# Queue orders, engine sides and bank places of a fused attention and MLP kernel drawn anew

## The chip, the cores and the metric

The kernel runs on one core of one Trainium2 chip. The metric is the device time of one execution in microseconds (us); less is better. The engines are TensorE (PE in the rows, PEld for its weight loads), VectorE (DVE), ScalarE (ACT), GpSimd (POOL) and SyncE (SP). GpSimd and SyncE do no arithmetic here, they issue DMAs: GpSimd those that change f32 into bf16 on the way ("casts"), SyncE the others.

## The reference

Attention with 8 batches, 8 heads, 576 positions, 64 columns a head. Heads 0 to 3 look at a local band, heads 4 to 7 at every 32nd position. Its output, as 4608 tokens by 512, goes through an MLP with a rational function between two products:

```python
mask_local = (rel >= 0) & (rel < 32)
mask_strided = (rel >= 0) & (pos[None, :] % 32 == pos[:, None] % 32)
scores = np.where(masks, q @ k.T / sqrt(64), -1e9)
x = (softmax(scores) @ v).transpose(0, 2, 1, 3).reshape(4608, 512)
h = x @ w_in                                   # 512 x 2048
P = a[0] + a[1] * h + a[2] * h**2 + a[3] * h**3
Q = 1 + abs(b[0]) * abs(h) + abs(b[1]) * h**2
out = (P / (Q + 1e-6)) @ w_out                 # 2048 x 512
```

## The kernel before

`graph` makes a list of 1239 operations in program order; an operation's place in this list is its number ("op 34"). Each names the tiles it reads and writes, from which its waits follow. `place` then takes five written queues, `ORDER`, one for each engine, each a permutation of that engine's op numbers, and `AT`, one digit for each use of PSUM, which gives its bank. `emit` issues every queue in that order with the semaphore waits that the tiles and banks ask for. An engine runs its queue strictly in order: an operation that waits holds up all behind it. `SIDE` is a string of letters, read one by one by `pick`, which say for each eviction, zero fill or `abs` whether ScalarE (a) or VectorE (d) does it. Nothing else decides the order.

**Attention.** Batch 0 is done in two parts, tokens 0 to 255 (part 0) and 256 to 575 (part 1); batches 1 to 7 whole. For batches 0 and 1 GpSimd casts q and k to SBUF, and TensorE turns them ("turn"); later batches are cast to a bf16 copy in DRAM and loaded with transposing DMAs by SyncE. V comes in two forms: vS for the strided heads and vl (tile vL) for the local ones; half of vl is a copy shifted by one block, which for batches from 1 on SyncE makes from the other half ("vsh"). Scores, row maximum, exponential, sum, norm, turn of P, product with V ("sav", "lav"), turn of the local result, and eviction to XT follow.

**MLP.** Ten chunks of tokens: 0 and 1 with 256 tokens each, 2 to 9 with 512 each. A chunk's 2048 middle columns are done in groups, two of 128x4096 elements for most chunks; chunk 0 has two of 128x2048, chunk 1 one of 128x4096, chunk 9 four (4096, 2048, 1024 and 1024 elements wide). "Group 3.0" is the first of chunk 3. For a group TensorE does the W_in steps, ScalarE or VectorE evicts h (L314), then `abs` (ScalarE L1116 or VectorE L1120), u1 and u2 (VectorE, L1123, L1126), ln and exp (ScalarE, L1131, L1136), and p1 to p5 and g (VectorE, L1140 to L1151), so ten long VectorE instructions or nine. W_out steps (L1168), an eviction to `os`, and an output DMA end a chunk.

**Numbers that the text uses.** Casts of GpSimd: 12 to 15 (q, k of part 0), 40 to 43 (q, k of part 1: 40 is q of the local heads), 22 to 25 and 44 to 47 (vS of the parts), 48 to 51 (vl of part 1), 34 and 35 (first and second half of W_in, columns 0 to 1023 and 1024 to 2047), 36 and 37 (halves of W_out), 150 to 153 (q, k of batch 1: 150 is q of the local heads), 210 to 213 (vS of batch 1), 214 to 217 (vl of batch 1). SyncE: 0 to 2 constants, 3 to 5 coefficients a, b and a constant, 218 and 219 vsh of batch 1. VectorE: 6 `babs` (absolute values of b, L308, which every u1 needs), 253 u1 of chunk 1, 1173 the last g. Evictions to XT: 93, 94, 99 (part 0), 320 and 325 (batch 1), 444 and 446 (batch 2), 563 and 565 (batch 3). `abs`: 252 (group 1.0), 363 (2.1), 459 (3.0), 578 (4.0), 939 (7.0), 1111 (9.0). Output evictions: 142 and 148 (chunk 0). TensorE: 144 is the first W_out step of the second 128 tokens of chunk 0; 1184 a pair of W_out matmuls of the last chunk that does not need op 1173 and in the new order stands behind two that do. Fills (L1258) are matmuls of zeros whose result nothing reads.

The casts and the order, in the code:

```python
weights(0, Win[:, :, 0:hw], w_in[:, 0:hw], T_win, "win")              # op 34
weights(1, Win[:, :, hw:2 * hw], w_in[:, hw:2 * hw], T_win, "win")    # op 35
P.op("dve", lambda e: e.scalar_tensor_tensor(coef[:, 6:8], coef[:, 4:6], -1.0, coef[:, 4:6],
     op0=Alu.mult, op1=Alu.max), "tiny", ("babs",), r=[T_co], w=[T_b])   # op 6
for ws, o in queues[e]:           # emit, one engine's queue
    for s, n in ws:
        eng.wait_ge(s, n)
    o.maker(eng).then_inc(o.sem, 16 if o.dma is not None else 1)
```

Of the kernel before, what the change touches and what calls it, by code (L numbers as in the profile page):

```python
# [208 lines left out]
def graph(nc, q, k, v, w_in, w_out, pa, pb, out):  # L209
# [1045 lines left out]
    P.op("dve", lambda e: e.memset(F.bitcast(f32)[:, :], 0.0), "mset64", ("fill", 0), w=[T_f])  # L1255
    for i in range(IDLE):
        BI = Banks(1)
# [5 lines left out]
IDLE = 36  # L1263
# [5 lines left out]
    "daadadadaaaadadaaddddadadaaaaadadaaaaaddaaadadadaaaddddddadaaaaddadaddddaaaadaaadddaaddaaaaaaaaaaaaa"  # L1269
    "aaaadddaaaaaaaaaaaaaaaadddaaaaaaaaaaaaaaaadaaaaaadaaaaaaaaaaaaaaaaaadaaaaaaaaaaadaaaaaadaaaaaaaaaaad"  # L1270
    "aaaaaadaaaaaaaaaaaaaaaaaaaaaaaaaaaadd"
# [24 lines left out]
    ),  # L1296
    "act": (
# [11 lines left out]
    ),  # L1309
    "dve": (  # L1310
# [80 lines left out]
```

## Time and profile before

| | |
|---|---|
| time, median of 3 runs | 353.13 us (352.05 to 354.07) |
| profiled execution, its own time | 349.6 us |
| its span | 347.8 us |
| busy: PE, DVE, ACT, POOL | 324.1, 323.2, 309.3, 74.6 us |
| moved by DMA | 44.68 MB, 128 GB/s |

The profile is one execution, and the span is the time from its first to its last instruction; the profiled execution's own time is a little longer. Busy times are sums over the span and tell nothing of where an engine is idle; the table by stretches does. A row "start us, us, what" gives the start, the length and the work. "Issue" as the cause of a wait means that the profile shows nothing that the engine waited for. "KB each" is what a DMA writes.

### The profile page before, as it was taken

How to read it: one execution, taken by the hardware profiler on the slowest of the kernel's cores; microseconds unless marked ns; L12 is line 12 of the kernel's file. 1: busy time of each engine (PE TensorE's matmuls, PEld its weight loads, DVE VectorE, ACT ScalarE, POOL GpSimd, SP SyncE). 2: the span in 40 equal slices, each digit the busy share in tenths (PEclk: the TensorE clock that was granted, in tenths of full speed). 3: DMA queues.
4: the chain of work that ended last, by engine and by line, in shares of the span. 5: the costliest groups of instructions: out<-in, count | busy, mean ns of one | idle time of the engine just before them, and what ended most of it. 6: DMA issues, size and time to landing. Idle time of an engine off the chain costs nothing.

```text
span 347.8 us, 9956 instructions
## 1 busy us (share of the span) xinstructions
PE 324.1 (93%) x4509; PEld 168.1 (48%) x4552; DVE 323.2 (93%) x291; ACT 309.3 (89%) x273; POOL 74.6 (21%) x112
## 2 busy tenths in 40 slices
PE   5886989999989999999999999999999999999895
PEld 2554667444544454455444454454454444444342
DVE  5783599999999999999999999999999999999994
ACT  8764389699989999899998998999979999999992
POOL 8980052160082062007004170000000000000000
PEclk9997899999999999999999999999999999999999
DMA  9999999995999999699999698701401002001023
GB/s 139 184 178 170 219 142 157 200 172 98 182 204 168 178 208 167 170 176 165 150 235 197 126 134 134 190 30 34 111 2 62 30 2 90 0 30 62 0 90 151
DMA packets 94313, 44.68 MB, mean 128 GB/s; under 512 B 79424, under 2 KB 87360, under 8 KB 93888
## 3 DMA queue, kind: packets, MB, share of 16 engines
q0 software_dynamic: 30528, 18.23, 40.1%
q1 hardware_dynamic: 63200, 25.69, 35.9%
q8 instruction: 35, 0.57, 0.7%
q10 hardware_dynamic: 544, 0.13, 0.2%
q14 instruction: 6, 0.05, 0.1%
HBM read 36.87 MB, written 16.52 MB: 154 GB/s over the span
## 4 chain that ended last, share of the span: by engine, by line
PE 46%; DVE 24%; ACT 15%; DMA 6%; POOL 5%; issue 3%; SPq 1%; DVEq 0%; POOLq 0%
PE ps L1168 19%; PE ps L1098 19%; DMA vL<-in_v_dram 4%; ACT u L1131 4%; ACT h L314 4%; DVE h L1151 4%; DVE u L1126 3%; ACT u L1136 3%; DVE z L1147 3%; DVE u L1123 2%; PE ps L683 2%; DVE z L1143 2%; DVE z L1149 2%; DVE z L1140 2%; DMA consts<-c_cst 2%
## 5 line engine op out<-in xcount | busy, mean ns | idle before, releaser
L1098 PE MATMUL ps<-XT,Win 128*128 128x512 bf16 (+1 forms) x626 | 133.1, 361 | 4.3 <-issue 3.3
L1168 PE MATMUL ps<-Wout,h 128*128 128x512 bf16 x547 | 129.3, 379 | 5.2 <-issue 2.9
L1098 PEld LDWEIGHTS ps<-XT,Win 128*128 128x128 bf16 x640 | 61.1, 99 | 63.7 <-ACT h L314 2.8
L314 ACT ACTIVATE h<-ps 128x1024 bf16<-128x1024 f32 (+1 forms) x78 | 71.2, 956 | 15.5 <-PE ps L1098 15.3
L1168 PEld LDWEIGHTS ps<-Wout,h 128*128 128x128 bf16 x576 | 53.3, 98 | 62.8 <-ACT h L314 1.6
L1131 ACT ACTIVATE u<-u 128x4096 bf16<-128x4096 bf16 (+2 forms) x22 | 66.3, 3012 | 1.1 <-DVE u L1126 1.1
L1136 ACT ACTIVATE u<-u 128x4096 bf16<-128x4096 bf16 (+2 forms) x22 | 66.1, 3010 | 0.1
L1116 ACT ACTIVATE z<-h 128x4096 bf16<-128x4096 bf16 (+2 forms) x16 | 46.0, 2878 | 1.7 <-DVE h L1151 1.3
L1143 DVE TENSOR_TENSOR z<-z,h 128x4096 bf16<-128x4096 bf16 (+2 forms) x21 | 41.5, 1978 | 0.2
L1126 DVE TENSOR_TENSOR u<-u,z 128x4096 bf16<-128x4096 bf16 (+2 forms) x21 | 41.5, 1977 | 0.2
L1147 DVE TENSOR_TENSOR z<-z,h 128x4096 bf16<-128x4096 bf16 (+2 forms) x21 | 41.4, 1979 | 0.2
L1151 DVE TENSOR_TENSOR h<-z,u 128x4096 bf16<-128x4096 bf16 (+2 forms) x21 | 41.4, 1979 | 0.2
L400 POOL DMA_DIRECT2D vL<-in_v_dram x32 | 24.4, 777 | 72.0 <-PE ps L1168 26.1
L391 POOL DMA_DIRECT2D vS<-in_v_dram x36 | 24.9, 708 | 27.0 <-PE ps L1168 18.2
L1123 DVE TENSOR_SCALAR u<-z,coef 128x4096 bf16<-128x4096 bf16 (+2 forms) x21 | 25.0, 1192 | 0.9 <-ACT z L1116 0.7
L1140 DVE TENSOR_SCALAR z<-h,coef 128x4096 bf16<-128x4096 bf16 (+2 forms) x21 | 24.7, 1178 | 0.2
L1145 DVE TENSOR_SCALAR z<-z,coef 128x4096 bf16<-128x4096 bf16 (+2 forms) x21 | 23.4, 1116 | 0.1
L1149 DVE TENSOR_SCALAR z<-z,coef 128x4096 bf16<-128x4096 bf16 (+2 forms) x21 | 23.3, 1117 | 0.1
L314 ACT ACTIVATE os<-ps 128x512 f32<-128x512 f32 x31 | 18.4, 618 | 0.6 <-PE ps L1168 0.6
L683 PEld LDWEIGHTS ps<-ptS,vS 18*64 18x64 bf16 (+1 forms) x1152 | 12.2, 108 | 10.7 <-issue 7.9
L1258 PE MATMUL ps<-F 128*128 128x512 bf16 x36 | 12.1, 426 | 5.1 <-DVE F L1255 4.1
L314 ACT ACTIVATE XT<-ps 128x576 bf16<-128x576 f32 (+7 forms) x30 | 16.1, 572 | 0.3 <-PE ps L1048 0.2
(109 smaller groups left out, 269.7 us busy)
## 6 DMA issues: line engine op xcount, KB each, us to landing
out_dram<-os SPq DMA_DIRECT2D x32, 256.0 KB, 2.5
qk<-in_k_dram POOLq DMA_DIRECT2D x12, 288.0 KB, 7.1
qk<-in_q_dram POOLq DMA_DIRECT2D x12, 288.0 KB, 6.6
Win<-in_moe_w_in_dram POOLq DMA_DIRECT2D x2, 1024.0 KB, 15.8
Wout<-in_moe_w_out_dram POOLq DMA_DIRECT2D x2, 1024.0 KB, 24.3
vS<-in_v_dram POOLq DMA_DIRECT2D x28, 72.0 KB, 5.7
vL<-in_v_dram POOLq DMA_DIRECT2D x28, 72.0 KB, 5.7
vL<-vL SPq DMA_DIRECT2D x14, 138.1 KB, 3.9
```

What stands on the lines that cost most here:

```text
L314: return lambda e: e.tensor_copy(o_(), i_()) if e_ == "dve" else e.activation(o_(), i_(), AF.Copy)
L1098: r = e.matmul(bank(ph, 512 * (s - s0) + n * i, n), Win[:, kk, f * 128:(f + 1) * 128], XT[:, kk, x0:x0 + n], start=(kk == 0), stop=(kk == ...
L1116: P.op(e_, lambda e, z=z, h=h, i=i, hp=hp: e.activation(z.t[:, hp * i:hp * i + hp, :], h.t[:, hp * i:hp * i + hp, :], AF.Abs), f"act_{hp * ...
L1123: dv(lambda e, z=z, u=u, G_=G_: e.tensor_scalar(u.t[:, 0:G_, :], z.t[:, 0:G_, :], b1_ap, b0_ap, op0=Alu.mult, op1=Alu.add), "ts2", "u1", r ...
L1126: dv(lambda e, z=z, u=u, G_=G_: e.tensor_tensor(u.t[:, 0:G_, :], u.t[:, 0:G_, :], z.t[:, 0:G_, :], op=Alu.mult), "tt", "u2", r=[z], m=[u])
L1131: lns.append(P.op("act", lambda e, u=u, i=i, hp=hp: e.activation(u.t[:, hp * i:hp * i + hp, :], u.t[:, hp * i:hp * i + hp, :], AF.Ln, bias ...
L1136: exs.append(P.op("act", lambda e, u=u, i=i, hp=hp: e.activation(u.t[:, hp * i:hp * i + hp, :], u.t[:, hp * i:hp * i + hp, :], AF.Exp, sca ...
L1140: dv(lambda e, z=z, h=h, G_=G_: e.tensor_scalar(z.t[:, 0:G_, :], h.t[:, 0:G_, :], a_ap[3], a_ap[2], op0=Alu.mult, op1=Alu.add), "ts2", "p1 ...
L1143: dv(lambda e, z=z, h=h, G_=G_: e.tensor_tensor(z.t[:, 0:G_, :], z.t[:, 0:G_, :], h.t[:, 0:G_, :], op=Alu.mult), "tt", "p2", r=[h], m=[z])
L1147: dv(lambda e, z=z, h=h, G_=G_: e.tensor_tensor(z.t[:, 0:G_, :], z.t[:, 0:G_, :], h.t[:, 0:G_, :], op=Alu.mult), "tt", "p4", r=[h], m=[z])
L1151: dv(lambda e, z=z, h=h, u=u, G_=G_: e.tensor_tensor(h.t[:, 0:G_, :], z.t[:, 0:G_, :], u.t[:, 0:G_, :], op=Alu.mult), "tt", "g", r=[z, u], ...
L1168: r = e.matmul(bank(po, 0, Fout), hf[:, j, m * 128:(m + 1) * 128], Wout[:, kk, :], start=(kk == 0), stop=(kk == NF - 1))
```

## The change

All five queues, the letters of `SIDE` and the digits of `AT` are replaced; four fills are added (`IDLE`). The operations, their tiles and their sizes are those of before. In GpSimd's queue op 34 moves from the 25th place to the 19th: what stood ahead of it and now stands behind are 152 and 150 (q of batch 1), 40, 48, 49, 51, 217, 211 and 212; what now stands ahead are 44, 45 and 47. Op 35 moves from the 32nd place to the 25th, op 36, the first half of W_out, from the 35th to the 36th, behind op 37 and all V of batch 1. In SyncE's queue 5, 4 and 3 move ahead of 218. 44 of the 237 letters differ; among them `abs` 363, 459, 578 and 1111 go from ScalarE to VectorE, 252 and 939 from VectorE to ScalarE, and nine evictions of 576 columns to ScalarE. The diff, cut to the heads of the queues:

```diff
-IDLE = 36
+IDLE = 40
...
     "pe": (
-        "1225 1208 1234 1226 1231 1216 1232 1218 1215 1219-1220 63 61 1233 1236 1224 66-68 56 58 70 1206 1222 "
-        "1238 1211 159 79 161 80-81 232 164-165 230 1204 83 166 1213 156 85 87 168 1235 77 95 154 227 224 "
-        "1207 1230 1212 75 177 1210 1221 175 89 178-179 222 91 237 181 98 173 1237 185 183 1205 90 220 92 193 "
-        "234 106 292 104 198 293-294 102 296 188 100 1203 187 190 189 121 119 249-250 123 305-307 301 125 303 "
-        "246 309 247 316 311 318 1228 313 243-244 321 240-241 324 326 315 317 138 354 334-335 355 331-332 337 "
...
+        "1224 1208 1238 1222 1242 1216 1226 1239 1205 1213 1212 1236 1228 1232 1241 1209 1221 56 58 1206 1217 "
+        "1214 1231 1220 79 1211 1234 1237 63 80 1207 81 61 234 1229 66-67 83 68 156 85 70 237 161 159 87 1210 "
+        "77 1227 1225 75 164 95 165 1203 166 98 224 168 89-92 1230 1223 102 104 100 154 106 177 175 178 173 "
+        "179 227 230 188 232 125 181 190 119 185 183 220 193 222 121 123 198 305 187 189 306 249-250 307 240 "
+        "292 309 241 293-294 243 246 296 244 247 144 313 311 138 321 145-146 301 303 147 315 139 317 324 316 "
...
     "act": (
-        "31 27 10 207 16 203 9 55 28 65 33 32 39 57 38 71 160 163 233 84 157 88 169 78 155 225 53 223 176 93 "
...
+        "31 27 19 33 57 59 38 9 39 235-236 84 71 158 86 200 160 238 88 225 169 94 103 53 101 155 108 231 126 "
...
     "dve": (
-        "18 17 7 21 20 11 201 19 1202 209 202 208 204-205 64 62 54 29 206 69 200 59-60 8 72-73 162 82 231 167 "
-        "74 86 158 96 170-171 226 97 172 76 228 180 239 52 238 174 194 196 195 197 236 235 107 199 295 103 "
-        "298 6 299-300 192 191 109-110 113-116 308 117 304 127-129 312 132 314 133 322-323 118 325 252-254 "
...
+        "21 209 18 7 1202 203 206 205 54 10 17 16 204 11 202 20 28 32 29 60 8 207 65 64 82 62 69 72-73 163 74 "
+        "55 157 239 78 162 76 96 208 97 167 226 99 170 93 52 6 105 171-172 107 176 174 201 180 109 228 110 "
+        "113 186 114 194 196 115 195 197 116 199 117 127-129 132 308 133-135 295 136 118 137 298 312 299-300 "
+        "322-323 302 253-254 320 257 142 148 258 418 259-261 421-422 262 429 423 341-342 345-347 363-364 "
...
     "pool": (
-        "15 14 12-13 42-43 25 211 152 41 40 212 46 151 150 50 23-24 51 49 48 22 153 217 34 216 47 214-215 45 "
-        "44 35 213 210 36-37 284 286 285 276 275 283 282 278-279 277 400 407 409 406 281 280 399 398 408 401 "
...
+        "12-13 44 15 14 153 41-43 46-47 24-25 151 50 45 23 22 34 48 152 51 49 40 35 216-217 150 212 37 213 "
+        "215 211 210 214 36 278 286 284 275 283 276 279-280 285 277 398 407 400 409 281 406 408 399 282 401 "
...
     "sp": (
-        "30 26 0 2 1 218 5 219 4 3 288-289 291 287 290 424 412 433 410 414 411 413 143 149 268 543 529 552 "
...
+        "30 26 5 0-1 4 2-3 218-219 289 291 288 287 290 143 424 412 433 411 410 414 413 149 531 552 274 533 "
```

## Rows read from the trace of the kernel before

**Rows 1.** The page, busy time (share of the span) x instructions of each engine.

```profile
PE 324.1 (93%) x4509; PEld 168.1 (48%) x4552; DVE 323.2 (93%) x291; ACT 309.3 (89%) x273; POOL 74.6 (21%) x112
```

**Rows 2.** The table by stretches: stretch, its length, busy time of each engine in it, granted TensorE clock, DMA share, GB/s.

```profile
30.70:37.50 6.80, 6.80 (x127) 5.01 (x128) 2.75 (x7) 1.61 (x4) 0.00 (x0) 0.50 1.18 197
37.50:44.60 7.10, 6.32 (x229) 4.78 (x228) 4.57 (x9) 4.33 (x5) 0.00 (x0) 1.00 1.28 221
44.60:62.80 18.20, 16.73 (x325) 12.81 (x323) 17.82 (x22) 16.18 (x17) 7.19 (x10) 1.00 1.07 148
62.80:342.00 279.20, 270.66 (x3343) 132.01 (x3384) 276.38 (x206) 264.12 (x214) 43.97 (x62) 1.00 0.67 118
```

**Rows 3.** The chain that ended last, up to 64 us: start, length, what. L473 is op 218, L308 op 6, the L1123 at 62.83 op 253.

```profile
18.87 14.54 DMA vL<-in_v_dram
33.42 0.76 SPq L473
...
36.10 6.57 DMA consts<-c_cst
...
42.69 0.16 DVE coef L308
...
62.83 1.36 DVE u L1123
```

**Rows 4.** Four casts of GpSimd, asked one by one: the issue (its length in ns, its start in us) and the time from its start to the landing, in us. The first cast of all; the first half of W_in; the second; the last half of W_out.

```profile
L383 POOL DMA_DIRECT2D XT<-in_k_dram x1: 758/758/758, 1.2 to 1.2; - x1
...
DMA to landing us min/median/max: 4.4/4.4/4.4
...
L478 POOL DMA_DIRECT2D Win<-in_moe_w_in_dram x1: 919/919/919, 16.2 to 16.2; - x1
...
DMA to landing us min/median/max: 13.7/13.7/13.7
...
L478 POOL DMA_DIRECT2D Win<-in_moe_w_in_dram x1: 948/948/948, 20.6 to 20.6; - x1
...
DMA to landing us min/median/max: 17.8/17.8/17.8
...
L478 POOL DMA_DIRECT2D Wout<-in_moe_w_out_dram x1: 1084/1084/1084, 23.4 to 23.4; - x1
...
DMA to landing us min/median/max: 26.5/26.5/26.5
```

**Rows 5.** The DMA issues: out<-in, engine, operation, count, KB each, median us to landing. XT is the staging place of q and k of batch 0 (128 KB part 0, 160 KB part 1; k has rows of the same size), h that of batch 1; vS of 32 and vL of 40 KB are those of the parts (vS of part 1 has 40 KB too), those of 72 KB belong to whole batches (vL has rows of the same size).

```profile
Win<-in_moe_w_in_dram POOLq DMA_DIRECT2D x2, 1024.0 KB, 15.8
...
vS<-in_v_dram POOLq DMA_DIRECT2D x28, 72.0 KB, 5.7
...
h<-in_q_dram POOLq DMA_DIRECT2D x2, 288.0 KB, 8.1
...
XT<-in_q_dram POOLq DMA_DIRECT2D x2, 160.0 KB, 6.5
...
XT<-in_q_dram POOLq DMA_DIRECT2D x2, 128.0 KB, 5.0
...
vL<-in_v_dram POOLq DMA_DIRECT2D x4, 40.0 KB, 7.2
...
vS<-in_v_dram POOLq DMA_DIRECT2D x4, 32.0 KB, 7.3
```

**Rows 6.** The timeline of TensorE: start, length, the W_in steps of 256 columns, x matmuls.

```profile
33.48 1.90 PE L1098 MATMUL ps<-XT,Win 128*128 128x256 bf16 x8
...
44.37 3.01 PE L1098 MATMUL ps<-XT,Win 128*128 128x256 bf16 x26 [0.38 <-DVE XT L314]
```

**Rows 7.** The waits of TensorE from 24 to 62.8 us: who, for what, us in total, times, longest.

```profile
PE ps L604 <- issue: 2.4, 1, 2.4
PE ps L1098 <- issue: 0.8, 1, 0.8
```

**Rows 8.** The groups of instructions by line and form, of VectorE and ScalarE: xcount | busy us, mean ns of one | idle before. L1120 and L1116 are `abs` on either engine, L314 an eviction of a bf16 and one of an f32 bank, L1147 p4 and L1145 p3 of a group of 2048.

```profile
L1120 DVE TENSOR_SCALAR z<-h 128x4096 uint16<-128x4096 uint16 x5 | 6.1, 1227 | 1.0 <-ACT h L314 0.9
...
L1147 DVE TENSOR_TENSOR z<-z,h 128x2048 bf16<-128x2048 bf16 x3 | 3.7, 1223 | 0.1
...
L1145 DVE TENSOR_SCALAR z<-z,coef 128x2048 bf16<-128x2048 bf16 x3 | 2.2, 749 | 0.0
...
L314 DVE COPY XT<-ps 128x576 bf16<-128x576 bf16 x5 | 2.2, 449 | 0.0
...
L314 DVE COPY os<-ps 128x512 f32<-128x512 f32 x1 | 0.7, 679 | 0.0
...
L1116 ACT ACTIVATE z<-h 128x4096 bf16<-128x4096 bf16 x11 | 39.9, 3629 | 1.1 <-DVE h L1151 0.9
```

**Rows 9.** The timeline of VectorE in the steady part: p1 of one group, p2 that reads it, u1 of another group, and p3 that does not read that u1.

```profile
287.36 1.34 DVE L1140 TENSOR_SCALAR z<-h,coef 128x4096 bf16<-128x4096 bf16 x1
288.74 2.29 DVE L1143 TENSOR_TENSOR z<-z,h 128x4096 bf16<-128x4096 bf16 x1
290.94 1.34 DVE L1123 TENSOR_SCALAR u<-z,coef 128x4096 bf16<-128x4096 bf16 x1
292.20 1.28 DVE L1145 TENSOR_SCALAR z<-z,coef 128x4096 bf16<-128x4096 bf16 x1
```

**Rows 10.** The timeline of TensorE after the last g: the last W_out matmuls, x matmuls.

```profile
342.06 2.12 PE L1168 MATMUL ps<-Wout,h 128*128 128x512 bf16 x9 [0.21 <-DVE h L1151]
```

More of the change, by code (lines that the diff above doesn't have):

```diff
@@ L1268 @@
 SIDE = (
-    "daadadadaaaadadaaddddadadaaaaadadaaaaaddaaadadadaaaddddddadaaaaddadaddddaaaadaaadddaaddaaaaaaaaaaaaa"
-    "aaaadddaaaaaaaaaaaaaaaadddaaaaaaaaaaaaaaaadaaaaaadaaaaaaaaaaaaaaaaaadaaaaaaaaaaadaaaaaadaaaaaaaaaaad"
-    "aaaaaadaaaaaaaaaaaaaaaaaaaaaaaaaaaadd"
+    "dadddadddaaadaddaaddddddaadadaaddaaaaadddadaaddddadaadadddddaaaddaaaaaadaaaaaaadadaaddaaaaaaaaaaadaa"
+    "aaaadaaaaaadaaaaaaaaaaadaaaaaadaaaaaaaaaaadaaaaaadaaaaaaaaaaaaaaaaaadaaaaaaaaaaadaaaaaaaaaaaaaaaaaad"
+    "aaaaaadaaaaaaaaaaaaadaaaaaaaaaaaaaadd"
 )
@@ L1338 @@
 AT = (
-    "1754500741153050067233777212510325060775164037066465145010432260530510532723203027602304664423306046"
-    "5666620440510030557522020246701205242466616201674016325234320461601427451533354626421465155003570730"
-    "76037016406252502274546211130324755113260"
+    "6340664177065467200320603321217474210056536755046234227524311752240014337006500025300234600763652540"
+    "4001664244102111413664426022273020405340356006452102512465325530611047046322644626246371032504532624"
+    "536527212421637352413274147246235576066337402"
 )
```

81 rows, old and new, of the table ORDER are left out of this document.

## Prediction

> **What bounds the kernel now.** I read the page first, then a table by stretches, then the chain that ended last, then the landings of GpSimd's casts. The page gives VectorE 323.2 us, 93% of the span [rows 1], an average over unlike stretches. The table [rows 2] splits it. From 62.8 to 342 VectorE works 276.38 of 279.20 us and TensorE 270.66: VectorE is the bound, TensorE close behind, and VectorE idles 2.8 us in all. From 44.6 to 62.8 it works 17.82 of 18.20. So the end is settled by two things: when VectorE's unbroken run starts, and how much work it then has. Before 44.6 it idles for long (in the 13.9 us from 30.7 on it works 7.3).
>
> Why so late? The chain [rows 3] answers: a cast of the second batch's V issued at 18.87 lands at 33.4; SyncE, waiting for it with op 218, only then gets to the coefficient loads 5, 4 and 3 behind it, whose last lands at 42.67; `babs` (op 6) follows on VectorE at 42.69, and from there the chain stays on VectorE and ScalarE up to 62.83, where u1 of chunk 1 (op 253) starts. I use op 253 as the milestone: all that varies much in this change lies ahead of it.
>
> **GpSimd's queue.** The casts land nearly in the order of issue, so a landing is the KB ahead of it over a pace. In the kernel before, the first cast lands at 1.2 + 4.4 = 5.6 and the first half of W_in at 16.2 + 13.7 = 29.9 [rows 4]. Between them lie 3 x 128 + 4 x 160 + 4 x 288 KB of q and k, 4 x 32 + 40 + 2 x 72 of the strided V, 4 x 40 + 72 of the local V, and the half itself, 1024: 3744 KB in 24.3 us, 154 KB/us [rows 4, 5]. From there to the last half of W_out (23.4 + 26.5 = 49.9) it is 3552 KB in 20.0 us, 177 KB/us. In the new order 17 casts with 1768 KB lie between the first cast and W_in's first half, then 568 KB (40, 152, 48, 51, 49) up to the second half:
>
> - first half: 5.6 + 2792/154 = 23.7 (was 29.9); second half: 23.7 + 1592/177 = 32.7 (was 20.6 + 17.8 = 38.4);
> - later than before: q of part 1 (op 40) at 27, q of the second batch (op 150, behind both halves) at 32.7 + 432/177 = 35.1, the last of the second batch's local V at 35.1 + 1456/177 = 43.3 (was 33.4), and W_out's first half, now last of all, at 43.3 + 1024/177 = 49.1, near the old end of 49.9, since the sum of the KB is the same.
>
> **The way to op 253 in the new order.** The coefficient loads now stand third, sixth and eighth on SyncE, ahead of 218, and wait for nothing: that wait goes. W_in's first half is there at 23.7, which is about when attention part 0 can deliver the 256 tokens (evictions 93, 94, 99; I walk its queues to 24 or 26). The first three W_in steps follow; the fourth stands behind the turn of op 40, so u1 of chunk 0 starts near 32 instead of 44.6. It does not run on unbroken: the other half of chunk 0 waits for W_in's second half. From 32.7 TensorE is the limit. To the last W_in step of chunk 1 its queue holds 12 steps of eight matmuls, 0.93 each (26 in 3.01 us [rows 6]), 11.1 us; some 18 short steps (masks, scores, turns, V products), which I put at 5 us; and waits of about 4 us (the turn of op 150 at 35.1, exponentials and evictions on ScalarE between the two turns of part 1). That gives 52.8. Then two evictions and one of P on ScalarE, 2.1 us, and `abs` of chunk 1 (op 252), which moves from VectorE to ScalarE, 3.63 instead of 1.23 [rows 8]: 58.5.
>
> What this walk lacks is TensorE waiting for nothing that the profile shows: 2.4 and 0.8 us between 24 and 62.8 [rows 7]. At zero, op 253 starts at 58.5; with all 3.2 us on the path, 61.7. As part falls in stretches that wait for data anyway, I take 2 us: 60.5, which is 2.3 us ahead of 62.83. VectorE has the room: ahead of op 253 the new order gives it some 4.5 us more (zero fills and casts taken from ScalarE), in time that it idles now. If that cover went, they would cost those 4.5 us.
>
> **What VectorE has left from op 253 on.** Added: `abs` of groups 2.1, 3.0, 4.0 and 9.0 at 1.23 each, +4.9 [rows 8]; an eviction of an f32 bank moved behind (op 148, 0.68 [rows 8]) and one moved from ScalarE (op 320; no row of that form; between 0.45 for bf16 and 0.68, I take 0.65). Removed: `abs` of 7.0, -1.23; five evictions of 576 columns (325, 444, 446, 563, 565) to ScalarE, -2.25 at 0.45; and the second half of chunk 0 (p3, p4, p5, g), now done ahead of op 253, -3.9 (p3 and p5 0.75 each, p4 and g 1.22 each [rows 8]). Sum -1.1. Against that, 34 instructions instead of 27 now read what the instruction right ahead wrote. Such a pair costs 0.12 more from start to start (287.36 to 288.74 against 290.94 to 292.20, 1.38 and 1.26 [rows 9]): +0.8. The remainder is the same to 0.3 us, -0.3. ScalarE gets some 8 us less in all; as it idles in this stretch already, that counts for nothing.
>
> **Tail.** After the last g (op 1173) one more pair of W_out matmuls is left in the new order (op 1184), 2 x 0.24 [rows 10]: +0.4. The four added fills stand in TensorE's queue where it waits for casts or evictions, and I take nothing for them; without that cover they cost at most 4 x 0.24 = 1 us.
>
> **Sum.** -2.3 - 0.3 + 0.4 = -2.2 us. The profiled execution took 349.6 us (span 347.8), 1% under the median of 353.13; 349.6 becomes 347.4, and 353.13 becomes 350.9.
>
> **The rivals.** One can't tell less than 0.5%, 1.8 us, from no change.
>
> *The start is repaid (no change).* The KB are the same, so what comes sooner at W_in comes later at q, k and V of the second batch, whose turns stand in TensorE's queue between the W_in steps. With the full 3.2 us of stalls on the path op 253 starts at 61.7, the sum is -1.1 - 0.3 + 0.4 = -1.0 us, and the time 352.1. For it: the last landing stays near 50, and VectorE is 98% busy from 44.6 on already. Against it: VectorE's long idling before 44.6. The Trainium skill ("DMA: Bandwidth & Descriptors", section "Issuing engines are not separate DMA queues") says that DMAs of all issuing engines run on the same 16 DMA engines and interleave; read strictly, an order buys no transfer time, and the gain would be nothing, 353.1. The trace agrees as to the sum of the landings, but its chain shows VectorE held up by a coefficient load of 1 KB behind a wait, which an order can mend.
>
> *W_out comes too late (slower).* In the new order the first W_out step, op 144, stands in TensorE's queue ahead of the turns and the V product of the second batch, and needs the half of W_out that is now last. I have TensorE there at 53 and the landing at 49.1. At the slower pace of 154 KB/us from 23.7 on, the 4504 KB behind W_in's first half land at 52.9; a tenth slower still, at 56.1. Each us past 53 holds `abs` of chunk 1 and op 253 by one. From 53 + 2.2 + 1.8 = 57 on the change is slower by over 0.5%: at 58, 353.13 - 2.2 + 5 = 355.9.
>
> *The clock falls at the wrong time (between).* Before, the granted clock was 0.50 from 30.7 to 37.5 [rows 2], after TensorE had stood still for 2.4 us [rows 7]; eight matmuls took 1.90 us in it [rows 6]. If such a stretch of 6.8 us falls after 32.7, where TensorE is now the limit, it costs up to 3.4 us: 350.9 + 3.4 = 354.3, no change.
>
> *More than expected (faster).* With no stall on the path op 253 starts at 58.5, -4.2; with a lighter ScalarE VectorE may also lose half of its 2.8 us of idle time: 347.6.
>
> **How the numbers follow.** Forecast and its faster neighbour, a gain of over 1.8 us: 0.51 (of that 0.13 for over 4). No change, by repayment, by the clock or by a different loss of the same size: 0.30, of which 0.04 for the strict rule. Slower: 0.19 (late W_out 0.09; the rest a new wait between the second batch's later V and TensorE, or banks redrawn badly, which the trace before cannot show; TensorE's 8.5 us of idle time after 62.8 [rows 2] bounds what banks can give back). The time is that of the likeliest, 350.9. The range runs from 347, the gain without stalls, to 355.5, W_out landing near 57.5.
>
> **What would show it.** W_in's halves landing near 24 and 33, the last of W_out near 50; no wait of VectorE for a coefficient load; u1 of chunk 0 near 32; op 253 (the first 4096-wide u1) at 58.5 to 62; from there to the last g 277 to 279 us, with VectorE idle under 4 us; the clock at 0.50 before 33 or not at all. Wrong it is if TensorE waits for W_out at op 144, if the clock is at 0.50 between 33 and 53, or if VectorE idles over 5 us after op 253.

## The result and the profile after

The changed kernel takes 354.12 us in the median of 20 runs, the kernel before 353.16 in as many of its own: 1.0 us more. The ratio is 1.0056 with a 95% interval of [1.0032, 1.0081], by which it is 2.0 us slower, a little over the 1.8 that the prediction could tell from no change. The ratio, here and below, leaves out executions more than 1.5% above the fastest of the same kernel, while the medians take all, and the execution profiled after is one of those left out. The forecast was 2.2 us faster.

The profiled executions lie further apart than the medians: 349.6 us before (3.5 under its median) and 356.47 after (2.3 over). The span grew by 354.0 - 347.8 = 6.2 us, more than the kernels differ. What is said of the size of the loss goes by the ratio and the medians, 1 to 2 us; the profiles say where time went in these two executions.

From the page after, the busy times and the queue that carries the engines' instructions (packets, MB, share):

```profile
PE 331.8 (94%) x4556; PEld 168.2 (48%) x4556; DVE 327.5 (92%) x293; ACT 302.6 (85%) x271; POOL 74.8 (21%) x112
...
q8 instruction: 35, 0.57, 0.7%
```

VectorE has 4.3 us more of work than in [rows 1]. The table by stretches answers [rows 2]. It is cut where TensorE stops and starts again (24.63, 26.41, 31.30, 35.31), at u1 of chunk 0 (42.03), at op 253 (67.16) and at the end of the last g (347.95). Columns as in [rows 2]: length, busy time and instructions of PE, PEld, DVE, ACT, POOL, granted clock, DMA share, GB/s.

```profile
0.00:24.63 24.63, 18.78 (x349) 9.94 (x349) 17.85 (x42) 12.83 (x20) 18.25 (x33) 1.00 1.18 161
24.63:26.41 1.78, 0.17 (x22) 0.07 (x10) 1.32 (x3) 0.57 (x1) 1.78 (x3) 1.00 1.75 138
26.41:31.30 4.89, 4.83 (x127) 3.47 (x127) 1.33 (x4) 2.26 (x3) 3.83 (x6) 0.74 1.37 195
31.30:35.31 4.01, 0.34 (x2) 0.00 (x0) 1.45 (x3) 0.00 (x0) 0.00 (x0) 0.89 1.90 103
35.31:42.03 6.72, 6.72 (x127) 4.80 (x128) 2.80 (x6) 3.75 (x4) 0.00 (x0) 0.75 1.35 192
42.03:67.16 25.13, 23.29 (x437) 16.51 (x435) 24.29 (x34) 22.95 (x25) 6.23 (x10) 1.00 1.09 133
67.16:347.95 280.79, 274.86 (x3509) 132.33 (x3507) 277.05 (x204) 259.02 (x218) 44.70 (x62) 1.00 0.65 119
```

The kernel before, cut at the same events (u1 of chunk 0 at 44.61, op 253, the last g):

```profile
0.00:21.30 21.30, 15.97 (x348) 9.42 (x348) 15.26 (x37) 17.28 (x25) 20.25 (x36) 1.00 1.22 161
21.30:27.70 6.40, 4.60 (x130) 2.77 (x128) 5.05 (x10) 4.05 (x6) 3.23 (x5) 1.00 1.43 189
27.70:44.61 16.91, 13.80 (x360) 10.19 (x361) 7.32 (x16) 6.52 (x10) 0.00 (x0) 0.80 1.40 197
44.61:62.82 18.21, 16.74 (x325) 12.81 (x324) 17.81 (x22) 16.17 (x17) 7.19 (x10) 1.00 1.07 149
62.82:342.01 279.19, 270.64 (x3343) 132.00 (x3384) 276.38 (x206) 264.12 (x214) 43.97 (x62) 1.00 0.67 118
```

Three readings. First, op 253 starts 67.16 - 62.82 = 4.3 us later, the rest to the last g takes 280.79 - 279.19 = 1.6 more, the tail 0.3 more: 6.2. Second, VectorE's work ahead of op 253 grew from 15.26 + 5.05 + 7.32 + 17.81 = 45.4 us to 49.0, and its idle time there did not shrink: 62.82 - 45.4 = 17.4 before, 67.16 - 49.0 = 18.1 after. Third, TensorE all but stops after 349 + 349 = 698 matmuls and weight loads for 1.8 us, and 254 later, after 952, for 4.0 us. Behind each stop the clock is at 0.50:

```profile
28.80:32.20 3.40, 2.84 (x14) 1.70 (x12) 1.13 (x3) 1.88 (x2) 1.44 (x2) 0.50 1.75 171
35.60:39.00 3.40, 3.40 (x29) 2.11 (x28) 0.15 (x1) 1.30 (x2) 0.00 (x0) 0.50 1.31 201
```

The chain, which answers [rows 3], shows the second stop as "issue", a wait for nothing that the profile shows:

```profile
24.80 1.62 issue
...
28.07 3.57 PE ps L1098 x19
31.64 3.67 issue
35.31 1.00 PE ps L1098 x5
```

The rows x19 and x5 are the first three W_in steps, eight matmuls each. The stop cuts through the middle of the third; no operation of the program begins there. [Rows 7] has the like of it, 2.4 and 0.8 us; here it is 3.7 and 1.6. The kernel before, too, stops after 475 + 476 = 951 instructions:

```profile
0.00:27.66 27.66, 20.57 (x475) 12.14 (x476) 20.31 (x46) 21.33 (x31) 23.49 (x40) 1.00 1.27 167
27.66:29.77 2.11, 0.00 (x1) 0.09 (x1) 0.00 (x0) 0.00 (x0) 0.00 (x0) 1.00 2.34 125
```

### The profile page after: what moved, and what is told of

Read it like the earlier page. It is cut to its first block, busy times and chain, and to the rows that moved or that the text cites. A ratio compares the mean times of both kernels' runs of the same rounds, so it can differ in the third digit from the quotient of the medians.

```text
span 354.0 us, 10000 instructions
## 1 busy us (share of the span) xinstructions
PE 331.8 (94%) x4556; PEld 168.2 (48%) x4556; DVE 327.5 (92%) x293; ACT 302.6 (85%) x271; POOL 74.8 (21%) x112
## 4 chain that ended last, share of the span: by engine, by line
PE 56%; DVE 26%; ACT 12%; issue 3%; DMA 2%; DVEq 0%; SPq 0%
PE ps L1098 23%; PE ps L1168 21%; ACT u L1136 3%; DVE h L1151 3%; ACT u L1131 3%; DVE z L1143 3%; PE ps L683 3%; DVE z L1147 3%; ACT h L314 2%; DVE z L1140 2%; DVE u L1126 2%; DMA qkT<-qk 2%; DVE u L1123 2%; DVE qkT L314 1%; DVE z L1149 1%
## 5 line engine op out<-in xcount | busy, mean ns | idle before, releaser
L1098 PE MATMUL ps<-XT,Win 128*128 128x512 bf16 (+1 forms) x640 | 136.1, 363 | 5.0 <-issue 3.7
L1168 PE MATMUL ps<-Wout,h 128*128 128x512 bf16 x576 | 135.3, 379 | 3.4 <-ACT os L314 1.3
L314 ACT ACTIVATE h<-ps 128x1024 bf16<-128x1024 f32 (+1 forms) x78 | 71.8, 973 | 16.7 <-PE ps L1098 16.5
L1116 ACT ACTIVATE z<-h 128x4096 bf16<-128x4096 bf16 (+2 forms) x14 | 38.6, 2762 | 3.9 <-DVE h L314 1.8
L1147 DVE TENSOR_TENSOR z<-z,h 128x4096 bf16<-128x4096 bf16 (+2 forms) x21 | 41.5, 1981 | 0.2
L400 POOL DMA_DIRECT2D vL<-in_v_dram x32 | 22.2, 697 | 49.7 <-PE ps L1168 44.3
L314 ACT ACTIVATE XT<-ps 128x576 bf16<-128x576 bf16 (+7 forms) x34 | 19.2, 589 | 8.8 <-PE ps L683 7.3
L1123 DVE TENSOR_SCALAR u<-z,coef 128x4096 bf16<-128x4096 bf16 (+2 forms) x21 | 24.9, 1187 | 0.4 <-ACT z L1116 0.2
L1145 DVE TENSOR_SCALAR z<-z,coef 128x4096 bf16<-128x4096 bf16 (+2 forms) x21 | 23.6, 1126 | 0.1
L314 ACT ACTIVATE os<-ps 128x512 f32<-128x512 f32 x30 | 18.5, 638 | 1.7 <-PE ps L1168 1.6
L450 POOL DMA_DIRECT2D qk<-in_k_dram x12 | 8.9, 743 | 43.3 <-PE ps L1098 23.8
L314 ACT ACTIVATE qkT<-ps 64x576 bf16<-64x576 bf16 (+6 forms) x16 | 10.0, 640 | 8.3 <-PE ps L563 4.4
```

The lines of the kernel that those rows point to most:

```text
L314: return lambda e: e.tensor_copy(o_(), i_()) if e_ == "dve" else e.activation(o_(), i_(), AF.Copy)
L1098: r = e.matmul(bank(ph, 512 * (s - s0) + n * i, n), Win[:, kk, f * 128:(f + 1) * 128], XT[:, kk, x0:x0 + n], start=(kk == 0), stop=(kk == ...
L1116: P.op(e_, lambda e, z=z, h=h, i=i, hp=hp: e.activation(z.t[:, hp * i:hp * i + hp, :], h.t[:, hp * i:hp * i + hp, :], AF.Abs), f"act_{hp * ...
L1123: dv(lambda e, z=z, u=u, G_=G_: e.tensor_scalar(u.t[:, 0:G_, :], z.t[:, 0:G_, :], b1_ap, b0_ap, op0=Alu.mult, op1=Alu.add), "ts2", "u1", r ...
L1147: dv(lambda e, z=z, h=h, G_=G_: e.tensor_tensor(z.t[:, 0:G_, :], z.t[:, 0:G_, :], h.t[:, 0:G_, :], op=Alu.mult), "tt", "p4", r=[h], m=[z])
L1168: r = e.matmul(bank(po, 0, Fout), hf[:, j, m * 128:(m + 1) * 128], Wout[:, kk, :], start=(kk == 0), stop=(kk == NF - 1))
```

## The experiments

Two theories at the start. **Supply**: TensorE stops because its instructions have not come; they come in blocks of 256 by DMA, among the casts. **Work**: VectorE has more to do, and when it starts matters little. A third question is what the coefficients were worth.

**The changed kernel, profiled again.** No edit.

> The changed kernel once more, for a second look at the same program: if the standstills are a property of the order, TensorE again stands still after its 698th and 952nd instruction, for 1.5 to 2.5 and 3 to 5 us, op 253 starts at 66 to 68, and from it to the last g it takes 279 to 281 us.

One row of its table by stretches, from 31.90 on:

```profile
31.90:35.02 3.12, 0.27 (x3) 0.00 (x0) 1.69 (x3) 0.80 (x1) 0.00 (x0) 0.91 1.66 105
```

It stops at the same places for 2.3 and 3.1 us, op 253 starts at 68.04, and the rest takes 280.0. Two kernels further down have the same start, since their edits come behind op 253: the one with small matmuls at its end and the one with four `abs` moved back. There u1 of chunk 0 starts at 37.3 and 40.1, op 253 at 65.7 and 66.2. So four profiles of this start have op 253 at 65.7 to 68.0, where the kernel before has 62.8 and, with its coefficient loads moved, 64.3. The late start belongs to this order. The standstills belong to the places in the count, their lengths vary. From op 253 to the last g the changed program took 280.8, 280.0 and, with the small matmuls behind it, 278.9 us: the 1.6 us more than before are not shown to belong to it.

The earliest of the four, from u1 of chunk 0 to op 253:

```profile
37.33:65.66 28.33, 25.74 (x437) 18.16 (x435) 24.56 (x34) 23.25 (x26) 6.23 (x10) 0.88 1.14 147
```

Its stops are shorter (1.1 and 1.0 us, and 1.7 at the next border, right behind u1), but the clock is at 0.50 from 38.6 to 45.4: with u1 4.7 us earlier, op 253 is only 1.5 us earlier.

**GpSimd held back.**

```diff
+    P.ops[35].deps[P.ops[92]] = 1
     P.place({e: list(_expand(t)) for e, t in ORDER.items()}, [int(x) for x in AT])
```

> The changed kernel, with one added wait: GpSimd issues the second half of W_in (op 35), and so all casts behind it, only when TensorE is through op 92 (the last V product of part 0, at 27.4). The casts ahead of it have landed by 28.3, so the DMA engines then have little to do until op 35's data move. Theory of supply: the block of instructions that came at 33.5 now comes before 30.5, TensorE stands still after its 952nd instruction for under 1.5 us instead of 4.1, and u1 of chunk 0 starts at 35 to 38 instead of 42.0; the second half of W_in lands some 5 us later (39), so the end can go either way. Rival: the standstill has another cause (a bank, a weight load, the cast of op 40): then it stays at 3.5 us or more at the same place.

Its table by stretches, cut at its own 698th instruction (24.64), 951st (28.37), u1 of chunk 0, op 253 and the last g, and then a stretch of low clock (the row from 24.64 to 28.37 is left out):

```profile
0.00:24.64 24.64, 19.57 (x347) 10.17 (x351) 17.82 (x42) 12.83 (x20) 15.30 (x28) 1.00 1.16 160
...
28.37:33.89 5.52, 5.23 (x126) 3.77 (x123) 4.53 (x9) 4.66 (x5) 5.52 (x9) 1.00 1.13 191
33.89:64.46 30.57, 26.49 (x438) 18.44 (x439) 24.74 (x34) 23.11 (x25) 6.80 (x11) 0.89 1.32 166
64.46:344.12 279.66, 274.50 (x3509) 132.26 (x3507) 277.02 (x204) 259.03 (x218) 45.60 (x62) 1.00 0.65 119
37.20:40.60 3.40, 3.40 (x49) 2.32 (x47) 0.41 (x1) 2.35 (x5) 0.00 (x0) 0.50 1.27 205
```

Both standstills are gone, and u1 of chunk 0 starts at 33.9, earlier than expected. The rows by DMA queue show what changed (packets, MB, time of the packets as a share of 16 engines, over 100% where packets overlap). First the changed kernel in the 5.5 us after its 698th instruction, then in the 1.65 after those (where the packet that ends the second stop runs), then the held kernel in the 2 us after its 698th:

```profile
q0 software_dynamic: 1446, 1.03, 146.2%
q14 instruction: 1, 0.01, 0.4%
```

```profile
q8 instruction: 1, 0.02, 5.7%
```

```profile
q0 software_dynamic: 377, 0.11, 53.4%
q8 instruction: 1, 0.02, 3.1%
```

In the changed kernel no packet of TensorE's queue (q8) runs from 26.41 to 31.95, while the casts (q0) keep the DMA engines at 146%; it runs after 31.95, and TensorE goes on at 35.31. With the casts held it runs within 2 us, before TensorE needs it. The page gives 35 such packets in 0.57 MB, 16 KB each, for 9112 matmuls and weight loads, 260 to a packet, and the stops lie 254 of those apart (a few instructions of the sequencer are not counted in them): blocks of about 256 instructions. The Trainium skill ("Runtime: NRT & Kernel Launch", section "Instruction fetch mechanics") has those sizes, 16 KiB blocks of 256 instructions fetched by a DMA queue of the sequencer's own, and calls the cost mostly hidden. The trace agrees as to the size; hidden it is not, with 4.0 us at one border.

The hold has its price. TensorE now waits 2.7 us for W_in's second half (landed 36.3, was 34.1), its clock falls to 0.50 in the stretch shown and again from 47.5 to 50.9, and op 253 starts at 64.5. Median 353.44 against 354.37 of the kernel before, ratio 1.0042 [1.0004, 1.008]: the earlier u1 bought little.

**The same, but sooner.** The wait is on op 89 instead of 92.

> As the kernel that held GpSimd at op 35 until TensorE was through op 92, but only until it is through op 89, two to three us earlier (24.8). Theory of supply: the block of instructions asked for at 24.6 is still ahead of the half of W_in and comes at 26.5 to 28; no standstill over 1 us at the 952nd instruction; u1 of chunk 0 at 33.5 to 36; the second half of W_in lands at 33.5 to 35 instead of 36.3, and op 253 starts at 61 to 63.5 instead of 64.5 (67.2 in the changed kernel). Time 2 to 4 us below the changed kernel. Rival: the later steps are held by something else (ScalarE, the half clock): op 253 stays at 64 to 66 and the time within 1 us of the other gate.

Its table by stretches, cut as above, and one stretch of low clock:

```profile
24.63:31.14 6.51, 5.39 (x148) 3.74 (x137) 2.50 (x7) 2.74 (x5) 4.72 (x7) 0.74 0.72 100
...
36.47:61.72 25.25, 23.48 (x438) 16.62 (x436) 24.34 (x34) 23.04 (x26) 6.24 (x10) 1.00 1.39 186
61.72:344.45 282.73, 276.28 (x3509) 133.09 (x3507) 277.32 (x204) 258.94 (x218) 44.94 (x62) 0.99 0.65 118
92.50:95.90 3.40, 3.40 (x43) 1.66 (x43) 2.50 (x4) 1.59 (x1) 0.00 (x0) 0.50 1.27 161
```

U1 of chunk 0 starts at 36.5, op 253 at 61.7, 5.4 us ahead of the changed kernel, as supply has it. The place of the 952nd instruction has no stop; one of 1.1 us is left at the 698th. In this execution the hold was not the sooner one: behind that stop the second half of W_in went out at 26.4 (26.1 with the wait on op 92) and landed at 36.1. What differs is that TensorE came to it later, had no wait for it, and kept its clock at 1.00 from 31.1 to 61.7.

But the span is 352.0, only 2.0 less. From op 253 to the last g it takes 282.7, 1.9 more, and the tail is 1.5 longer. The place of the first, in its chain:

```profile
...
84.32 6.34 DMA qkT<-qk
...
90.70 0.42 PE ps L620 x2
```

TensorE, now earlier, waits 1.8 us for the third batch's q and k, whose load (op 412) stands on SyncE behind the transposing of P (op 424); then its clock is at 0.50 from 92.5 to 95.9. Median 353.11 against 354.04, ratio 1.0014 [0.9975, 1.0054].

**That load moved forward**, with the same hold:

```diff
-        "30 26 5 0-1 4 2-3 218-219 289 291 288 287 290 143 424 412 433 ...
+        "30 26 5 0-1 4 2-3 218-219 289 291 288 287 290 143 412 424 433 ...
```

> The kernel with the gate at op 89, and on SyncE the load of the third batch's strided q and k (op 412) ahead of the transposing of the second batch's P (op 424) instead of behind it. In the trace of the gated kernel TensorE waits for op 412's load from 88.9 to 90.7, the granted clock then falls to 0.50 from 92.5 to 95.9, and VectorE is idle 5.4 us from op 253 to the last g, where the first gated kernel had 2.6. Theory: op 412 is issued at 80 to 82 instead of 84.3, the wait and the half clock go, and the time falls by 1.5 to 3 us below the kernel with the gate alone, under the kernel before. Rival: op 424's transposing, now later, holds TensorE's product of P and V instead, and the time is the same or up to 2 us longer.

From its chain:

```profile
87.49 2.24 issue
89.73 0.46 PE ps L683 x32
```

The rival came: op 412 goes out at 83.3 (80 to 82 were expected), and op 424, now behind it, lands at 89.6; TensorE, which has come to the product of P and V (L683), stands still up to 89.73, and the clock is at 0.50 from 90.0 to 93.4. Of 283.3 us from op 253 on VectorE idles 6.2. The median is 352.42 against 354.01, ratio 0.9968 [0.9923, 1.0014]: the lowest of the study, not told apart from the kernel before. SyncE needs 2.7 to 2.9 us to issue the one load and 1.3 to 2.3 for the other, and at this point both are wanted at once.

**Supply without casts.** In the changed kernel, 640 small matmuls of zeros behind everything else:

```diff
+    for i in range(16):
+        BI = Banks(1)
+        def tiny(e, BI=BI):
+            for _ in range(40):
+                o = e.matmul(bank(BI, 0, 8), F[:, :], F[:, 0:8], start=True, stop=True)
+            return o
+        P.op("pe", tiny, "idle", ("tiny", i), r=[T_f], w=[BI])
```

> The changed kernel with 640 more matmuls of zeros (8 columns each, nothing reads them) behind the last W_out matmul, 1280 more instructions of TensorE, five blocks of 256, at a time when no cast moves. It measures the supply by itself; its own time is of no interest. Theory of supply: in the cast phase a block started no sooner than 5.2 to 8.9 us after the one before. If the casts are what makes the blocks late, TensorE gets through 256 of these in 3.5 to 5.5 us here, with standstills under 2 us. If blocks are always this slow, it stands still at each of the borders and 256 of them take 7 us or more.

Two blocks of them in its table by stretches (a few instructions that straddle a cut are counted twice):

```profile
350.34:353.60 3.26, 3.26 (x134) 3.26 (x132) 0.00 (x0) 0.00 (x0) 0.00 (x0) 0.85 0.03 5
353.60:357.02 3.42, 3.42 (x134) 3.42 (x132) 0.00 (x0) 0.00 (x0) 0.00 (x0) 0.50 0.02 5
...
```

256 instructions pass in 3.4 us, block after block, with TensorE busy throughout. In the cast phase the changed kernel needed 1.78 + 4.89 = 6.7 and 4.01 + 6.72 = 10.7 us for as many, larger ones, and stood still for 1.8 and 4.0 of them. Without casts no block was late.

**Fewer fills.** 30 of the 33 fills ahead of op 106 left out (they compute nothing):

```diff
-IDLE = 40
+IDLE = 10
-        "1224 1208 1238 1222 1242 1216 1226 1239 1205 1213 1212 1236 1228 1232 1241 1209 1221 56 58 1206 1217 "
+        "56 58 79 63 80 81 61 234 66-67 83 68 156 85 70 237 161 159 87 77 75 164 95 165 1203 166 98 ... "
```

> The changed kernel, with 30 of the 33 fills that TensorE's queue has ahead of op 106 (the fourth W_in step of chunk 0) left out. In the trace of the changed kernel TensorE stands still for 1.8 us after 698 and for 4.1 us after 952 of its matmuls and weight loads, with nothing that it waits for; in the kernel before it stands still after 951 too. Theory of supply: its instructions come in blocks of 256 by a DMA that queues among the casts (16 KB packets of the queue called instruction, one at 32.01, just ahead of the restart), so the place of the standstill is a place in the count. With 60 instructions fewer all four W_in steps of chunk 0 come ahead of it: u1 of chunk 0 starts at 33 to 37 instead of 42.0, the standstill comes right behind op 106, op 253 starts 2 to 6 us earlier, and the time falls by 1 to 4 us. Rival, the clock: without fills TensorE is idle for longer, the granted clock is at 0.50 ahead of 28 us, and the time rises. Rival, VectorE's work alone: the start matters little, the time stays within 0.7 us.

Its table by stretches, from the start to each of two stops:

```profile
0.00:26.02 26.02, 14.77 (x346) 10.10 (x349) 17.91 (x42) 12.82 (x20) 18.72 (x34) 1.00 1.18 165
0.00:41.18 41.18, 27.43 (x603) 19.16 (x603) 25.80 (x57) 19.61 (x28) 23.64 (x40) 0.92 1.32 167
```

The two long stops (2.7 and 3.9 us) come after 695 and 1206 instructions, 511 apart: places in the count, 60 instructions further on in the work. At the border between there is no stop; TensorE came to it late enough, it seems, for the block to be there. For the time I was wrong. u1 of chunk 0 starts at 40.1 instead of 33 to 37, op 253 at 69.5, and the median is 359.05 against 354.37, ratio 1.0225 [1.0149, 1.0301]. The rival of the clock came. These are the same masking matmul of 512 columns (op 83) at 14.3 us in the changed kernel, and at 14.4 without fills; the third row is one of the same form in the changed kernel's stretch at 0.50:

```profile
14.32 0.39 PE L782 MATMUL ps<-ng,IDN 128*128 128x512 bf16 x1
```

```profile
14.41 0.61 PE L782 MATMUL ps<-ng,IDN 128*128 128x512 bf16 x1
```

```profile
38.60 0.59 PE L746 MATMUL ps<-M,IDN 128*128 128x512 bf16 x1
```

Without them TensorE did 3.0 us of work up to 12 us and ran at the low level. The Trainium skill ("TensorE: Matmul & The Clock Gate", section "Part 1: The HAM clock gate") has an idle array at 1.2 GHz instead of 2.4; the durations agree with that, although the column of the granted clock reads 1.00 there; its first record in this trace comes at 25 us. Ahead of op 253 the clock is then at 0.50 from 28.4 to 35.2 and from 45.5 to 48.9, 10.2 us where the changed kernel has 6.8. How much of the loss that makes was not measured apart.

**The turns moved back**, with all fills kept:

```diff
-        pe: ... 61 234 1229 ... 70 237 161 ... 98 224 168 89-92 1230 1223 102 104 100 154 106 177 175 178 ...
+        pe: ... 61 1229 ... 70 161 ... 98 168 89-92 1230 1223 102 104 100 154 106 224 234 175 237 177 178 ...
```

(and the six evictions behind 155, 107 and 176 on their engines).

> The changed kernel, with the turns 224, 234 and 237 of the second batch (64 matmuls and weight loads that stand ahead of the W_in steps in TensorE's queue), and their six evictions, moved behind the fourth W_in step of chunk 0 (op 106). All fills stay. Theory of supply: the border after 952 instructions then falls behind op 106, so u1 of chunk 0 starts at 32 to 36 instead of 42.0, with the standstill of some 4 us right behind. But the border that holds the last W_in step of chunk 1 (the 1932nd instruction) comes no sooner, since the count up to it is the same: op 253 starts at 64 to 67, and the time falls by 0 to 2 us. Rival: if the start of u1 of chunk 0 were what counts, op 253 would start at 59 to 62 and the time fall by 4 us or more.

Its table by stretches, up to the first stop, and the longest stretch of low clock:

```profile
0.00:24.77 24.77, 21.24 (x348) 11.20 (x349) 17.01 (x41) 10.68 (x16) 18.89 (x33) 0.86 1.18 161
...
38.30:55.30 17.00, 15.20 (x228) 10.71 (x228) 10.16 (x17) 11.07 (x16) 0.00 (x0) 0.50 1.01 118
```

It stops after 697 instructions, and the four W_in steps then run through (29.7 to 36.4); the stop expected right behind them did not come. U1 of chunk 0 starts at 45.3 instead of 32 to 36: the clock is at 0.50 for 30.7 us ahead of op 253, and the turns, back to back, wait for each other's evictions. Op 253 starts at 74.0, and the time is 361.88 against 354.04, ratio 1.0259 [1.0203, 1.0315]. For the count this says little; for the clock much.

**Coefficients alone**, in the kernel before:

```diff
-        "30 26 0 2 1 218 5 219 4 3 288-289 291 ...
+        "30 26 0 2 1 5 4 3 218-219 288-289 291 ...
```

> The kernel before, with one edit: on SyncE the coefficient loads 5, 4 and 3 stand ahead of op 218. By the prediction's reading of the chain they were what held the start: babs then comes before 20 us instead of at 42.7. If they were the bound by much, u1 of chunk 0 starts several us before 44.62 and op 253 before 61; time 2 us down or more. The rival: the abs of chunk 0 on ScalarE ended at 43.97 in the kernel before, 0.65 us ahead of u1, so the coefficients were only just the last of several; then u1 starts at about 44.0, op 253 at 62 to 63, and the time moves by less than 1 us.

`babs` (op 6) runs at 43.09, right behind the instruction ahead of it, so it waits no more; u1 of chunk 0 starts at 45.70, 0.03 after `abs` (op 108) ends on ScalarE. Median 354.18 against 354.37, ratio 1.0041 [0.9985, 1.0097]. That wait was worth nothing that can be told: in the kernel before it was the last of several that ended within 0.7 us, since `abs` of chunk 0 ended at 43.97 there:

```profile
42.06 1.91 ACT L1116 ACTIVATE z<-h 128x2048 bf16<-128x2048 bf16 x1
```

The profiled execution (span 356.1) is the slowest of its twelve. Its clock is at 0.50 from 24.7 to 38.4 (30.7 to 37.5 before), so its u1 is not dated by the edit alone. Op 253 starts at 64.33. The rest takes 286.0 instead of 279.2, with the clock at 0.50 from 65.7 to 69.1 and from 137.4 to 140.8; the second lies across these two rows of its table:

```profile
120.00:140.00 20.00, 17.83 (x362) 9.00 (x360) 19.72 (x16) 17.66 (x12) 7.86 (x12) 0.93 1.22 206
140.00:150.00 10.00, 10.00 (x116) 4.85 (x115) 7.30 (x6) 8.60 (x5) 0.00 (x0) 0.96 0.84 159
```

**Four `abs` back on ScalarE**, in the changed kernel:

```diff
-        act: ... 343 359 439 ... 455 475 ... 571 777 ... 1107 1110 1068 ...   dve: ... 347 363-364 ... 373 459-460 ... 492 578 679 ... 1072 1111 1073 ...
+        act: ... 343 359 363 439 ... 455 459 475 ... 571 578 777 ... 1107 1110-1111 1068 ...   dve: ... 347 364 ... 373 460 ... 492 679 ... 1072-1073 ...
```

> The changed kernel, with the abs of groups 2.1, 3.0, 4.0 and 9.0 (ops 363, 459, 578, 1111) back on ScalarE, each right behind the last eviction of its group. It takes 4 x 1.23 = 4.9 us off VectorE and puts 4 x 3.63 = 14.5 us on ScalarE. If VectorE's work from op 253 on sets the end, as the prediction has it, the time falls by 3 to 5 us. If TensorE has become the bound (busy 50.00 of 50 us from 150 to 200 in the trace of the changed kernel), or ScalarE's abs comes late to u1, it falls by less than 1 us or rises.

A row of VectorE's waits from op 253 on (us in total, times, longest):

```profile
DVE u L1123 <- ACT z L1116: 10.6, 5, 3.2
```

Most of it is u1 of three groups (3.2, 3.1 and 2.3 us). The second case came: u1 stands still for the slower `abs`, what waits for it on TensorE and ScalarE slips, and the time is 369.69 against 354.37, ratio 1.0499 [1.0413, 1.0585]. VectorE's work did fall, from 277.0 to 273.1 us, and its idle time rose to 22.7. So the price of an `abs` here was not its length but what waited for it.

**`abs` of chunk 1 on VectorE**, with the hold on op 89:

```diff
-        act: ... 248 314 252 304 ...   dve: ... 323 302 253-254 320 ...
+        act: ... 248 314 304 ...       dve: ... 323 302 252-254 320 ...
```

> The kernel with the gate at op 89, and the abs of chunk 1 (op 252) back on VectorE as in the kernel before, right ahead of op 253. The prediction put its 3.63 us on ScalarE on the path to op 253. If that is the path, op 253 starts 1 to 2.4 us earlier and the time falls by as much. If VectorE is full there anyway (24.34 us of work in the 25.25 from u1 of chunk 0 to op 253), its 1.23 us only come on top: op 253 starts 0 to 1.5 us later and the time is 0 to 1.5 us longer.

One row of its table by stretches, from u1 of chunk 0 to op 253:

```profile
37.91:64.30 26.39, 24.55 (x473) 17.05 (x471) 25.51 (x35) 20.12 (x25) 6.23 (x10) 1.00 1.34 179
```

From u1 of chunk 0 to op 253 it is 26.39 us instead of 25.25, with VectorE busy 25.51 instead of 24.34: the 1.2 us only came on top. VectorE is full there. Op 253 starts 2.6 us later, not 0 to 1.5: the first stop is 1.8 us instead of 1.1 in this execution, and u1 of chunk 0 itself starts 1.4 us later. The time, 353.70 against 354.01, ratio 0.999 [0.9953, 1.0027], can't be told from that of the kernel with the hold alone.

## Why the prediction was wrong

**GpSimd's queue: right.** W_in's halves landed at 24.4 and 34.1 (forecast 23.7 and 32.7), q of the second batch at 38.0 (35.1), the last of its local V at 46.9 (43.3), W_out's first half last of all at 51.2 (49.1): up to 3.6 us late, in the order forecast.

**The coefficient wait: right that it goes, wrong about its worth.** I read the chain's one path as the reason for the late start. The chain names what ended last, not how close the next was behind; in the kernel before that was 0.7 us, and the kernel with the loads moved alone is no faster.

**"U1 of chunk 0 starts near 32": the step that failed.** It started at 42.0. W_in and the tokens were there (first step at 28.1). What the walk had as "waiting for nothing that the profile shows", a term of 2 us for the whole way, came as 1.6 and 3.7 us, 5.3 in sum, ahead of the fourth W_in step, and behind each of them the clock was at 0.50 for 3.4 us (28.8 to 32.2, 35.6 to 39.0). The 6.2 us that TensorE worked in these cost it some 3 more; that is an estimate, from the 1.90 and 0.93 us of eight matmuls at either level [rows 6]. Both make 8 of the 10 us. The rows of it were before me [rows 7], but I took the 3.2 us as a loose loss instead of asking what they were: the kernel before stops at 951 too, for 2.1 us. With the casts held back the stops went and u1 started at 33.9: here the count of instructions up to a step, and the casts in flight when its block was fetched, set the date. W_in earlier brought TensorE to the border in the thick of them.

**"VectorE has the room": failed with it.** VectorE's work ahead of op 253 rose by 3.6 us (forecast 4.5). Of 49.0 us of work ahead of op 253, 24.3 stand behind u1 of chunk 0 in VectorE's queue, where the kernel before has 17.8. With u1 at 32 and op 253 at 60.5 there was room for them; from 42.0 on they run with 0.8 us of idle time and set op 253 to 67.2. That is where the expected gain went in this profile. The kernel with the hold on op 89 bears the walk out: with the standstill down to 1.1 us and u1 at 36.5, op 253 starts at 61.7, the upper end of the 58.5 to 61.7 of the prediction. But an early u1 is not enough. Where it came at 33.9 and 37.3, 6.8 us at half clock followed, and to op 253 it took 30.6 and 28.3 us.

**The remainder and the tail: nearly right.** VectorE's work from op 253 on rose by 0.7 us (forecast -0.3), its idle time from 2.8 to 3.7, the tail by 0.3 (0.4).

**The rivals.** TensorE did not wait for W_out: op 144 ran at 61.6, W_out had landed at 51.2. The clock fell behind the stops, half of it ahead of 32.7 and half of it after, where the prediction had put its rival; the time of that rival, 354.3, lies near the 354.12 measured, by luck, since it has no late instructions. Repayment holds in a form that I had not seen: even a start 1.1 us ahead of the kernel before (61.7 against 62.8) brought no more than 353.11 against 354.04, where from there the third batch's loads come too late for TensorE. "The slower cases" had no place for a standstill on instructions; it stood in the forecast as a term of 2 us instead of as a case.

**Left open.** The two profiles differ by 6.2 us, the medians by 1.0, the ratio by 2.0. The kernel before was profiled near its fastest; whether its usual execution starts as early, or loses time behind op 253 as that with the coefficients moved did (286.0 us, its slowest), is not known. So how much of the 1 to 2 us lies ahead of op 253 is not shown. That the packet of instructions waits behind packets of casts in the DMA engines, and not for something else that the casts keep busy, was not tried apart.

## What to carry to other kernels

Where TensorE stands still for "issue", count its instructions up to there: stops some 256 apart while casts ran were late instruction blocks here. A pause in the casts mended them, at the price of the transfers behind it. A chain that ended last shows one path; ask how far behind the next one was before pricing the wait that heads it. Work moved into another engine's idle time is free only if the idle time stays where it was: price it a second time with the milestone ahead of it 10 us late.

## What the runs showed of the hardware

- TensorE's instructions came in 16 KB packets, one for about 256 matmuls and weight loads. With casts in flight a border cost up to 4.0 us; without them 256 instructions passed in 3.4 us with none.
- Behind stops of TensorE the granted clock was at 0.50: in the changed kernel from 28.8 and 35.6 (stops up to 26.4 and 35.3), in those with the hold on op 89 from 92.5 and 90.0 (stops up to 90.7 and 89.7). One stop of 1.1 us had it behind it too (25.9; 0.50 from 27.6 to 31.1).
- With fills at the very start a matmul at 14 us took 0.39 us, without them 0.61.
